# An adaLN block with a spectral filter: second layer norm's roots as a power on GpSimd, the Silu table loaded in the filter, one modulation later, one PSUM ring, a new order of the way back

## The chip, the cores and the metric

The kernel runs on one core of one Trainium2 chip. The metric is device time in microseconds of one execution; a kernel's time is the median of its runs. Before the change three runs gave 273.46, 274.78 and 277.28 us, median 274.78.

The engines by the profile's names: PE is TensorE's matmul, PEld its weight load, DVE is VectorE, ACT is ScalarE, POOL is GpSimd, SP issues nearly all transfers. Each engine works through its own instructions in order and waits for the others by semaphores.

## What is computed

One block on x of 2048 rows and 640 columns, in bf16, with six modulation vectors from a row c:

```python
mod = (_silu(c) @ w_mod).reshape(c.shape[0], 6, 1, -1)
sa, ca, ga, sb, cb, gb = ...
h = _layernorm(x, axis=-1) * (1 + ca) + sa
x = x + ga * _A_ref(h, A_w_r, A_w_i)     # irfft2(rfft2(h) * (w_r + 1j*w_i))
h = _layernorm(x, axis=-1) * (1 + cb) + sb
x = x + gb * _B_ref(h, B_w_gate, B_w_up, B_w_down)   # (silu(h@w_gate) * (h@w_up)) @ w_down
```

The layer norm has no weights: (x - m) / sqrt(v + 1e-5). The feed-forward is 1728 wide, that is 13 chunks of 128 and one half chunk of 64 (chunk 13 in the code).

## The kernel before

The 2048 rows lie on 128 partitions as 16 tiles. The stages follow one another: the first layer norm with the forward transforms (to about 36 us of the profile), the filter, 17 units of frequencies (to about 70 us), the way back, which overlaps with the second layer norm and the start of the feed-forward (to about 106 us), and the feed-forward in four blocks of four tiles (to the end).

Scheduling is by hand. In each stage a string of short words, `plan`, is walked and each word calls a step; every engine gets its instructions in the order of that string. For the way back (lines 799 to 805) the words are: `s` the inverse transform over rows of one tile on PE (L657, ten matmuls into `va`), `V` its copy to SBUF on ACT (L664), `d` the inverse transform over columns on PE (L670, five matmuls into `oab`), `x` the residual sum on DVE with its row sum (L673), `n` the mean on DVE (L677), `q` the square with its row sum on ACT (L681), `rt` the roots of tiles 0 to 3 (L683 to L687), `xn` and `xa` the normalised tile on DVE and ACT (L711, L714), `T` a pair of tiles turned on PE (L722), `f` its five affine pieces on ACT and DVE (L726, L728), `gA` chunk 13 (L749 and its Silu on ACT), `g`, `z`, `m` a chunk's ten matmuls (L762), its Silu on ACT (L767) and the product on DVE (L771), `mA` the product of chunk 13, `mb` and `mt` the columns of the gate gb and their turn into a row, `w` the fold of gb into a chunk of W_down on DVE (L788), `N` the roots of tiles 4 to 7, and `wm` the load of ACT's Silu table (L690).

Tiles 0 to 3 take their root as Sqrt on ACT and a reciprocal on DVE. The tiles behind them take it on DVE as an integer guess and three Newton steps, twelve short instructions (`ln2_newton`, L692 to L705). ACT holds one table of functions at a time: Silu is loaded at the start, Sqrt behind it (L358), Silu again at L690.

The modulations sb and cb are taken as columns on PE at the end of the filter (`mods_sb`, `mods_cb`, 25 matmuls of one column each, L221), and ACT writes them to `modcols` and `one_p_cb`; the affine pieces read both.

PSUM is a ring of four slots of two banks. The filter's pool, `ps2`, ends with the filter, and the way back has one of its own, `ps3`. A slot can be written again when the reader of the tile that held it four tiles earlier is done: a copy `V` for a `va`, a sum `x` for an `oab`, a product `m` for a chunk.

SBUF is shared by tags. W_gate (`Wg`) takes the place of `wm_g`, from which the columns of ga and cb are taken; `wm_gb` takes that of `wm_sb`; W_down (in `late`) takes that of the filter's weights `Wb`, which the products of the filter read. A transfer into such a place waits for the last reader of what was there. SP issues in this order at the end of the filter: `Wg` in two parts (L603), `wm_gb` (L629), W_down in three (L634, L636), later the turned gate's row to DRAM and its spread back to all partitions (L236, L242).

Of the kernel before, what the change touches and what calls it, by code (L numbers as in the profile page):

```python
# [104 lines left out]
def adaln_block_kernel(  # L105
# [28 lines left out]
    KIt = const.tile([P, 7, NI], BF16, name="KIt")  # L134
    modcols = const.tile([P, 2, NC5], F32, name="modcols")
# [270 lines left out]

    with tc.tile_pool(name="ph2", bufs=2) as ph2, \
         tc.tile_pool(name="ps2", bufs=4, space=bass.MemoryType.PSUM) as ps2:
        B2all = big.tile([P, 8, NR, 128], BF16, name="B2all", tag="gt")
# [162 lines left out]

        def rinv_gate(_):
# [13 lines left out]
        def loads(i):  # L587
            if i == 0:
                nc.sync.dma_start(wm_g[:, :, 0:D], wm_v[:, :, 2 * D:3 * D])
                nc.sync.dma_start(Rinv_sb[:], Rinv_dram)  # L590
            elif i == 1:
                nc.sync.dma_start(wm_g[:, :, D:2 * D], wm_v[:, :, 4 * D:5 * D])
            elif i == 2:
                nc.sync.dma_start(wm_sb[:], wm_v[:, :, 3 * D:4 * D])
            elif i == 3:
                nc.sync.dma_start(Htab[:], H_dram)
            elif i == 4:
                nc.sync.dma_start(Wu[:], B_w_up[:, 0:FFM].rearrange("(dp c5) f -> dp c5 f", dp=P))
                for k, w_ in enumerate((B_w_gate, B_w_up)):
                    nc.sync.dma_start(Wp13[:, :, 64 * k:64 * k + 64], w_[:, FFM:FF].rearrange("(dp c5) f -> dp c5 f", dp=P))  # L600
            else:
                for f0, f1 in ((0, 640), (640, FFM)):
                    nc.sync.dma_start(Wg[:, :, f0:f1], B_w_gate[:, f0:f1].rearrange("(dp c5) f -> dp c5 f", dp=P))  # L603

# [23 lines left out]
        wm_gb = big.tile([P, NC5, D], BF16, name="wm_gb", tag="wsb")
        nc.sync.dma_start(wm_gb[:], wm_v[:, :, 5 * D:6 * D])  # L629

    late = big.tile([P, NT * D + NFC * D], BF16, name="late", tag="wb")
# [44 lines left out]
    def ln2_mean(t):  # L676
        nc.vector.tensor_scalar(mean2[:, t:t + 1], xsum[:, t:t + 1], 1.0 / D, None, ALU.mult)  # L677

    def ln2_square(t):
        junk = ph4.tile([P, D], BF16, name="junk2", bufs=1)  # L680
        nc.scalar.activation(junk[:], x1[:, t, :], ACT.Square, scale=-1.0, bias=mean2[:, t:t + 1], accum_out=sq2[:, t:t + 1])  # L681

    def ln2_root(_):  # L683
        nc.scalar.activation(rstd2[:, 0:4], sq2[:, 0:4], ACT.Sqrt, bias=eps_t[:], scale=1.0 / D)
# [4 lines left out]
    def silu_table(_):  # L689
        nc.scalar.activation(warm[:], rstd2[:, 3:4], ACT.Silu)  # L690

    def ln2_newton(a, b):  # L692
        I32 = mybir.dt.int32
        n = b - a
        v = ph4.tile([P, 8], F32, name="veps")[:, 0:n]
        nc.vector.tensor_scalar(v, sq2[:, a:b], 1.0 / D, EPS, ALU.mult, ALU.add)
        yi = ph4.tile([P, 8], I32, name="rs_yi")[:, 0:n]
        nc.vector.tensor_single_scalar(yi, v.bitcast(I32), 1, ALU.arith_shift_right)
        nc.vector.tensor_scalar(yi, yi, -1, 0x5F3759DF, ALU.mult, ALU.add)
        y = yi.bitcast(F32)  # L700
        tt = ph4.tile([P, 8], F32, name="rs_t")[:, 0:n]
        for it in range(3):
            nc.vector.tensor_tensor(tt, y, y, ALU.mult)
            nc.vector.scalar_tensor_tensor(tt, tt, -0.5, v, ALU.mult, ALU.mult)
            nc.vector.scalar_tensor_tensor(rstd2[:, a:b] if it == 2 else y, tt, 1.5, y, ALU.add, ALU.mult)  # L705

    def ln2_xn(t):
        sc, tl = divmod(t, 4)
        if tl == 0 and sc:
            xn2s[sc] = big.tile([P, 4, D], BF16, name="xn2c", tag="rs")  # L710
        nc.vector.tensor_scalar(xn2s[sc][:, tl, :], x1[:, t, :], mean2[:, t:t + 1], rstd2[:, t:t + 1], ALU.subtract, ALU.mult)  # L711

# [64 lines left out]

    def gb_mods(_):
        mg_ps = ring("mg_ps")
        mod_cols(mg_ps[:, 0], wm_gb)  # L780
        nc.scalar.copy(g_col[1][:], mg_ps[:, 0, 0:NC5])

# [26 lines left out]

    done = 8  # L810
    folds = {8: (4, 5, 6), 9: (7,), 10: (8,), 11: (9, 10, 11), 12: (12, 13)}
    for sc in range(4):
# [139 lines left out]
```

## Time and profile before

| | us |
|---|---|
| median of three runs | 274.78 (273.46 to 277.28) |
| the profiled execution | 273.99 |
| its span, from the first instruction to the last | 272.2 |
| granted TensorE clock | 1.00 |

A stage's reading: busy time by engine in a stretch against its length. In a row of the timeline the first number is the start, the second the time from there to the end of the last of its instructions, and the bracket names the idle time of that engine just before and the instruction that ended it. Ends of matmuls are modelled and include a tail in which the next one already runs, so the rate of PE is read from starts. From 106 us on, the stretches look alike: a chunk every 2.16 us, then the products with W_down.

### The profile page before, as it was taken

Reading aid. Unit: us, or ns where it says so; the run is one execution under the profiler, and the core shown is the slowest. Engines: PE = TensorE matmul, PEld = TensorE weight load, DVE = VectorE, ACT = ScalarE, POOL = GpSimd, SP = SyncE. Lnnn points to the kernel's source line nnn. Section 1 sums busy time; section 2 is a strip of 40 time slices with the busy share of each in tenths; the row PEclk is TensorE's granted clock in tenths of the full one; section 3 lists DMA queues with packets and bytes.
Section 4 is the critical chain, followed back from the end, with each engine's and each line's share of the span. In section 5 each row is a group of like instructions: output and inputs, shape, how many; then the busy total and the mean of one; then the engine's idle time right before and its main releaser. Section 6 shows DMA issues by size and latency. Waiting matters only on the chain.

```text
span 272.2 us, 5350 instructions
## 1 busy us (share of the span) xinstructions
PE 260.6 (96%) x2190; PEld 169.0 (62%) x2190; DVE 151.0 (55%) x359; ACT 121.9 (45%) x221; POOL 22.0 (8%) x44
## 2 busy tenths in 40 slices
PE   6999989899987999999999999999999999999995
PEld 5888859798886555456744446654445664444663
DVE  2589989698577568892434553434334343333142
ACT  5499589798599985622032233022222203232000
POOL 3368910000000000000000000000000000000000
PEclk9999999999999999999999999999999999999999
DMA  7999359989499100031210005110004021000011
GB/s 241 333 327 276 131 106 246 281 203 287 102 377 355 29 11 26 0 63 37 72 35 12 0 0 96 51 55 3 12 0 88 11 72 34 12 0 0 0 52 48
DMA packets 35423, 27.80 MB, mean 102 GB/s; under 512 B 18117, under 2 KB 32710, under 8 KB 35270
## 3 DMA queue, kind: packets, MB, share of 16 engines
q1 hardware_dynamic: 35396, 27.46, 36.3%
q8 instruction: 17, 0.28, 0.4%
q14 instruction: 8, 0.07, 0.1%
q10 hardware_dynamic: 2, 0.00, 0.0%
HBM read 20.37 MB, written 2.62 MB: 84 GB/s over the span
## 4 chain that ended last, share of the span: by engine, by line
PE 78%; DMA 3%; ACT 3%; DVE 2%; issue 1%; SPq 0%; ACTq 0%; DVEq 0%
PE gu L762 41%; PE oa L863 20%; DMA wm_g<-in_w_mod_dram 3%; PE yps L493 2%; PE va L657 2%; PE gu L749 2%; DVE late L673 1%; PE m_ps L221 1%; PE oa L850 1%; PE oab L670 1%; PE wps L581 1%; ACT junk L681 1%; PE ob L863 1%; PE xps L446 1%; PE xps L447 1%
## 5 line engine op out<-in xcount | busy, mean ns | idle before, releaser
L771 DVE TENSOR_TENSOR AT<-gu,sg 128x512 bf16<-128x512 f32 x52 | 35.9, 690 | 54.4 <-ACT sg L767 54.4
L762 PE MATMUL gu<-h2T_all,Wg 128*128 128x512 bf16 x260 | 64.6, 380 | 0.0
L762 PE MATMUL gu<-h2T_all,Wu 128*128 128x512 bf16 x260 | 64.6, 380 | 0.0
L767 ACT ACTIVATE sg<-gu 128x512 f32<-128x512 f32 x52 | 31.0, 596 | 70.0 <-PE gu L762 68.5
L863 PE MATMUL oa<-late,AT 128*128 128x320 bf16 x403 | 56.1, 300 | 0.0
L863 PEld LDWEIGHTS <-AT 128*128 128x128 bf16 x429 | 40.8, 98 | 17.2 <-issue 1.4
L762 PEld LDWEIGHTS <-Wu 128*128 128x128 bf16 x260 | 25.4, 98 | 30.7
L762 PEld LDWEIGHTS <-Wg 128*128 128x128 bf16 x260 | 25.1, 98 | 29.4
L877 DVE TENSOR_TENSOR xo<-oa,late 128x320 bf16<-128x320 f32 x31 | 20.0, 695 | 29.3 <-PE oa L850 16.2
L673 DVE SCALAR_TENSOR_TENSOR late<-oab,x_sb 128x640 bf16<-128x640 f32 x16 | 14.1, 884 | 9.9 <-PE oab L670 9.8
L751 ACT ACTIVATE sg<-gu 64x512 f32<-64x512 f32 x4 | 2.3, 586 | 34.8 <-PE gu L749 34.8
L300 POOL TENSOR_SCALAR Gs<-Gtab,rstd 128x256 bf16<-128x256 bf16 x15 | 13.8, 922 | 12.3 <-DVE rstd L295 11.0
L312 DVE SCALAR_TENSOR_TENSOR Z<-rtile,vm,z 128x640 bf16<-128x640 f32 x16 | 13.9, 874 | 0.4 <-PE z L307 0.3
L681 ACT ACTIVATE junk<-late,mean 128x640 bf16<-128x640 bf16 x16 | 13.2, 827 | 0.3
L325 ACT CAST A_sb<-aps 128x650 bf16<-128x650 f32 x16 | 11.1, 706 | 2.5 <-PE aps L321 2.3
L276 ACT COPY early<-t1ps 128x640 bf16<-128x640 bf16 x13 | 9.0, 692 | 6.3 <-DVE ssq L285 3.1
L461 ACT CAST X<-xps 128x640 bf16<-128x640 f32 x16 | 10.9, 718 | 1.3 <-PE xps L454 0.6
L657 PE MATMUL va<-Htab,Ep 128*128 128x128 bf16 x160 | 10.7, 219 | 0.8 <-ACT VT L664 0.4
L664 ACT CAST VT<-va 128x640 bf16<-128x640 f32 x16 | 10.4, 701 | 1.4 <-PE va L657 1.4
L657 PEld LDWEIGHTS <-Ep 128*128 128x128 bf16 x160 | 9.9, 118 | 1.0 <-issue 0.8
L479 DVE TENSOR_TENSOR PP<-X,Wb 128x768 bf16<-128x768 bf16 x16 | 8.8, 552 | 2.7 <-ACT ga_col L559 2.3
L493 PE MATMUL yps<-identb,PP 128*128 128x128 bf16 x130 | 9.9, 219 | 0.3 <-ACT Y L504 0.3
(292 smaller groups left out, 340.9 us busy)
## 6 DMA issues: line engine op xcount, KB each, us to landing
x_sb<-in_A_x_dram SPq DMA_DIRECT2D x8, 320.0 KB, 5.8
out_dram<-xo SPq DMA_DIRECT2D x15, 160.0 KB, 1.8
Wu<-in_B_w_up_dram SPq DMA_DIRECT2D x1, 2080.0 KB
late<-in_B_w_down_dram SPq DMA_DIRECT2D x1, 2080.0 KB
wm_g<-in_w_mod_dram SPq DMA_DIRECT2D x2, 800.0 KB, 5.1
Wb<-in_A_w_r_dram SPq DMA_DIRECT2D x1, 1284.0 KB, 10.2
Wb<-in_A_w_i_dram SPq DMA_DIRECT2D x1, 1284.0 KB
Wg<-in_B_w_gate_dram SPq DMA_DIRECT2D x1, 1280.0 KB
```

Of the source, the lines that this page charges most:

```text
L300: e.tensor_scalar(Gss[t][:, 0:2], Gtab[:, t], rstd1[:, t:t + 1], None, ALU.mult)
L312: nc.vector.scalar_tensor_tensor(Zs[t][:].rearrange("p r q -> p (r q)"), rv, vm[:, t, 1:2], held.pop(("z", t))[:, 0:D], ALU.mult, ALU.add)
L325: (nc.vector.tensor_copy if t in A_DVE else nc.scalar.copy)(A_sb[:, :, t, :, :], i)
L493: nc.tensor.matmul(yf[:, 128 * j:128 * j + 128], lhsT=PP[:, cp, 0:128] if u == 16 else PP[:, cp, 0:128, j], rhs=identb[:], start=(cp == 0) ...
L657: nc.tensor.matmul(vf[:, 128 * r:128 * r + 128], lhsT=Ep[:, t, 65 - 65 * g:193 - 65 * g, r], rhs=Htab[:, t, g, :], start=(f == 1 and r in ...
L673: nc.vector.scalar_tensor_tensor(x1[:, t, :].rearrange("p (r a) -> p r a", r=NR), VTs.pop(t).rearrange("p (r a) -> p r a", r=NR), 1.0, x_s ...
L681: nc.scalar.activation(junk[:], x1[:, t, :], ACT.Square, scale=-1.0, bias=mean2[:, t:t + 1], accum_out=sq2[:, t:t + 1])
L762: nc.tensor.matmul(o, lhsT=w_[:, c5, fc * 128:(fc + 1) * 128], rhs=h2T_all[:, sc % 2, :, c5, :], start=(c5 == 0), stop=(c5 == NC5 - 1))
L767: nc.scalar.activation(gus[fc][1][:], gus[fc][0][:, 0, :], ACT.Silu)
L771: nc.vector.tensor_tensor(AT[:, fc, :], gu[:, 1, :], sg[:], ALU.mult)
L863: nc.tensor.matmul(o, lhsT=AT[:, fc, tl * 128:(tl + 1) * 128], rhs=Wd_sb[:, fc, h * 320 + d0:h * 320 + d0 + n], start=(fc == 0 and not ear ...
L877: nc.vector.tensor_tensor(xos[tl][:, h * 320:(h + 1) * 320].rearrange("p (a r) -> p a r", r=NR), ps[0][0].rearrange("p (a r) -> p a r", r= ...
```

## The change

Tiles 0 to 3, 4 to 7 and 8 to 15 get their roots from one step on GpSimd, an add of epsilon and a power with the exponent -0.5. So that the squares come out already divided by 640, the square's scale becomes -1/sqrt(640), and the mean is written twice, once as it is and once divided by sqrt(640), by one DVE instruction with a table `over_d`. The Silu table is loaded in the filter, ahead of the product of unit 6 and the columns of ga. The columns of sb and cb leave the filter's order; sb's come first in the way back, cb's behind the eighth `d`. The ring `ps2` stays for the rest of the kernel, and `ps3` goes. `wm_gb` is loaded behind sb's columns and `Wg` behind cb's, so that W_down is now ahead of both in SP's queue. The order of the way back is written anew. A copy of cb's columns that nothing read goes.

```diff
+    nc.gpsimd.memset(over_d[:, 0:1], 1.0 / D)
+    nc.gpsimd.memset(over_d[:, 1:2], D ** -1.5)
+    nc.gpsimd.memset(mhalf[:], -0.5)
...
-    with tc.tile_pool(name="ph2", bufs=2) as ph2, \
-         tc.tile_pool(name="ps2", bufs=4, space=bass.MemoryType.PSUM) as ps2:
+    ps2 = ctx.enter_context(tc.tile_pool(name="ps2", bufs=4, space=bass.MemoryType.PSUM))
+    with tc.tile_pool(name="ph2", bufs=2) as ph2:
...
-        def mods_cb(_):
-            m = mods(wm_g, 1)
-            nc.scalar.copy(modcols[:, 1, :], m)
-            nc.scalar.add(one_p_cb[:], m, 1.0)
-
-        def mods_sb(_):
-            nc.scalar.copy(modcols[:, 0, :], mods(wm_sb, 0))
+        def silu_table(_):
+            nc.scalar.activation(warm[:], eps_t[:], ACT.Silu)
...
-            "Xe9 P6 ga P7 Y4 Y5 y4 P8 y5 E3 X10 e3 Xe10 gt m0 E4 Y6 E5 y6 P9 Y7 e4 T16 W3 E6 e5 y7 t16 L4 X11 e6 E7 Y8 Xe11 "
+            "Xe9 wm P6 ga P7 Y4 Y5 y4 P8 y5 E3 X10 e3 Xe10 gt m0 E4 Y6 E5 y6 P9 Y7 e4 T16 W3 E6 e5 y7 t16 L4 X11 e6 E7 Y8 Xe11 "
...
-            "Xe15 Y13 Y16 y13 E10 E11 y16 P15 Y14 e10 E12 e11 y14 e12 E13 e13 Y15 E16 y15 m1 E14 m2 e16 E15 e14 m3 e15 m4 sb "
-            "Ri cb L5 "
+            "Xe15 Y13 Y16 y13 E10 E11 y16 P15 Y14 e10 E12 e11 y14 e12 E13 e13 Y15 E16 y15 m1 E14 m2 e16 E15 e14 m3 e15 m4 Ri "
...
-        wm_gb = big.tile([P, NC5, D], BF16, name="wm_gb", tag="wsb")
-        nc.sync.dma_start(wm_gb[:], wm_v[:, :, 5 * D:6 * D])
...
-    ps3 = ctx.enter_context(tc.tile_pool(name="ps3", bufs=4, space=bass.MemoryType.PSUM))
...
     def ln2_mean(t):
-        nc.vector.tensor_scalar(mean2[:, t:t + 1], xsum[:, t:t + 1], 1.0 / D, None, ALU.mult)
+        nc.vector.tensor_scalar(mean2[:, t], over_d[:], xsum[:, t:t + 1], None, ALU.mult)
 
     def ln2_square(t):
         junk = ph4.tile([P, D], BF16, name="junk2", bufs=1)
-        nc.scalar.activation(junk[:], x1[:, t, :], ACT.Square, scale=-1.0, bias=mean2[:, t:t + 1], accum_out=sq2[:, t:t + 1])
+        nc.scalar.activation(junk[:], x1[:, t, :], ACT.Square, scale=-1.0 / D ** 0.5, bias=mean2[:, t, 1:2], accum_out=sq2[:, t:t + 1])
+
+    def ln2_power(a, b):
+        nc.gpsimd.tensor_scalar(sq2[:, a:b], sq2[:, a:b], EPS, None, ALU.add)
+        nc.gpsimd.tensor_tensor(rstd2[:, a:b], sq2[:, a:b], mhalf[:, 0:b - a], ALU.pow)
 
     def ln2_root(_):
-        nc.scalar.activation(rstd2[:, 0:4], sq2[:, 0:4], ACT.Sqrt, bias=eps_t[:], scale=1.0 / D)
-        nc.vector.reciprocal(rstd2[:, 0:4], rstd2[:, 0:4])
-        nc.vector.scalar_tensor_tensor(nb2[:], mean2[:, 0:4], -1.0, rstd2[:, 0:4], ALU.mult, ALU.mult)
+        ln2_power(0, 4)
         xn2s[0] = big.tile([P, 4, D], BF16, name="xn2c", tag="rs")
...
+    def ln2_bias(_):
+        nc.vector.scalar_tensor_tensor(nb2[:], mean2[:, 0:4, 0], -1.0, rstd2[:, 0:4], ALU.mult, ALU.mult)
...
     plan = (
-        "s0 V0 s1 V1 s2 V2 s3 V3 s4 V4 d0 x0 n0 s5 V5 q0 d1 x1 n1 s6 q1 V6 d2 x2 s7 V7 d3 x3 n2 q2 n3 q3 d4 x4 s8 V8 d5 "
-        "x5 n4 n5 rt s9 V9 xn0 xn1 s10 V10 xa3 xn2 d6 T0 x6 s11 f0 V11 T1 f1 s12 V12 n6 d7 x7 n7 s13 V13 wm gA g0 q4 z0 "
-        "d8 x8 n8 m0 s14 V14 q5 g1 z1 d9 x9 n9 m1 s15 V15 q6 q7 g2 z2 d10 x10 n10 m2 mA mb q8 q9 g3 z3 d11 x11 n11 m3 "
-        "mt q10 g4 z4 d12 x12 n12 m4 d13 x13 n13 q11 w0 g5 z5 d14 x14 n14 m5 q12 d15 x15 n15 w1 g6 z6 m6 q13 w2 w3 q14 "
-        "g7 z7 m7 N q15 "
+        "sb s0 sx s1 V0 s2 d0 s3 x0 V1 s4 V2 d1 n0 d2 V3 s5 x1 V4 x2 q0 s6 d3 V5 n1 V6 d4 q1 s7 V7 x3 d5 n2 x4 q2 x5 mb "
+        "n3 d6 s8 s9 mx x6 d7 q3 rt x7 V8 n4 cb V9 nb s10 s11 xn2 xn0 cx V10 V11 d8 xa3 xn1 mt x8 T0 s12 T1 f0 s13 V12 f1 "
+        "d9 V13 s14 x9 n5 V14 s15 V15 d10 x10 gA n6 q4 q5 d11 d12 x11 g0 n7 d13 z0 x12 m0 w0 n8 n9 g1 q6 g2 q7 n10 z1 x13 "
+        "mA q8 q9 q10 w1 z2 d14 m1 g3 g4 n11 z3 x14 m2 n12 z4 q11 q12 n13 d15 x15 g5 m3 z5 n14 q13 m4 N g6 n15 q14 z6 q15 "
+        "w2 g7 m5 m6 w3 z7 m7 "
     )
     for w in plan.split():
         n = w.rstrip("0123456789")
         steps[n](int(w[len(n):] or 0))
+        if w == "sb":
+            wm_gb = big.tile([P, NC5, D], BF16, name="wm_gb", tag="wsb")
+            nc.sync.dma_start(wm_gb[:], wm_v[:, :, 5 * D:6 * D])
+        if w == "cb":
+            Wg = big.tile([P, NC5, FFM], BF16, name="Wg", tag="wg")
+            for f0, f1 in ((0, 640), (640, FFM)):
+                nc.sync.dma_start(Wg[:, :, f0:f1], B_w_gate[:, f0:f1].rearrange("(dp c5) f -> dp c5 f", dp=P))
```

In the new order `sx`, `cx` and `mx` are ACT's writes of sb, 1 + cb and gb, and `nb` is the bias for ACT's `xa`.

More of the change, by code (lines that the diff above doesn't have):

```diff
@@ L134, in adaln_block_kernel @@
     KIt = const.tile([P, 7, NI], BF16, name="KIt")
-    modcols = const.tile([P, 2, NC5], F32, name="modcols")
+    modcols = const.tile([P, 1, NC5], F32, name="modcols")
     one_p_cb = const.tile([P, NC5], F32, name="one_p_cb")
@@ L140, in adaln_block_kernel @@
     neg1 = const.tile([P, 1], F32, name="neg1")
+    over_d = const.tile([P, 2], F32, name="over_d")
+    mhalf = const.tile([P, 8], F32, name="mhalf")
     ssq, vm = (const.tile([P, NT, 2], F32, name=n) for n in ("ssq", "vm"))
@@ L600, in loads @@
                     nc.sync.dma_start(Wp13[:, :, 64 * k:64 * k + 64], w_[:, FFM:FF].rearrange("(dp c5) f -> dp c5 f", dp=P))
-            else:
-                for f0, f1 in ((0, 640), (640, FFM)):
-                    nc.sync.dma_start(Wg[:, :, f0:f1], B_w_gate[:, f0:f1].rearrange("(dp c5) f -> dp c5 f", dp=P))
         Y_ACT = (1, 3, 5, 7, 9, 11, 13, 15)
@@ L619, in adaln_block_kernel @@
                  "W": lambda i: negate(*WCOLS[i], neg_dve), "m": lambda i: mirror(*MCOLS[i]), "ga": mods_ga, "gt": ga_turn,
-                 "Ri": rinv_gate, "cb": mods_cb, "sb": mods_sb}
+                 "Ri": rinv_gate, "wm": silu_table}
         for w in plan.split():
@@ L624, in adaln_block_kernel @@
                 Wu = big.tile([P, NC5, FFM], BF16, name="Wu", tag="a")
-            if w == "L5":
-                Wg = big.tile([P, NC5, FFM], BF16, name="Wg", tag="wg")
             steps[n](int(w[len(n):] or 0))
-        wm_gb = big.tile([P, NC5, D], BF16, name="wm_gb", tag="wsb")
-        nc.sync.dma_start(wm_gb[:], wm_v[:, :, 5 * D:6 * D])
     late = big.tile([P, NT * D + NFC * D], BF16, name="late", tag="wb")
@@ L639, in adaln_block_kernel @@
     ph3 = ctx.enter_context(tc.tile_pool(name="ph3", bufs=6))
-    ps3 = ctx.enter_context(tc.tile_pool(name="ps3", bufs=4, space=bass.MemoryType.PSUM))
-    xsum, mean2, sq2, rstd2 = (const.tile([P, NT], F32, name=n) for n in ("xsum", "mean2", "sq2", "rstd2"))
+    xsum, sq2, rstd2 = (const.tile([P, NT], F32, name=n) for n in ("xsum", "sq2", "rstd2"))
+    mean2 = const.tile([P, NT, 2], F32, name="mean2")
     nb2 = const.tile([P, 4], F32, name="nb2")
@@ L645, in ring @@
     def ring(name):
-        return ps3.tile([P, 2, 512], F32, name=name, tag="f")
+        return ps2.tile([P, 2, 512], F32, name=name, tag="f")
     def flat(ps):
@@ L676, in ln2_mean @@
     def ln2_mean(t):
-        nc.vector.tensor_scalar(mean2[:, t:t + 1], xsum[:, t:t + 1], 1.0 / D, None, ALU.mult)
+        nc.vector.tensor_scalar(mean2[:, t], over_d[:], xsum[:, t:t + 1], None, ALU.mult)
     def ln2_square(t):
         junk = ph4.tile([P, D], BF16, name="junk2", bufs=1)
-        nc.scalar.activation(junk[:], x1[:, t, :], ACT.Square, scale=-1.0, bias=mean2[:, t:t + 1], accum_out=sq2[:, t:t + 1])
+        nc.scalar.activation(junk[:], x1[:, t, :], ACT.Square, scale=-1.0 / D ** 0.5, bias=mean2[:, t, 1:2], accum_out=sq2[:, t:t + 1])
+    def ln2_power(a, b):
+        nc.gpsimd.tensor_scalar(sq2[:, a:b], sq2[:, a:b], EPS, None, ALU.add)
+        nc.gpsimd.tensor_tensor(rstd2[:, a:b], sq2[:, a:b], mhalf[:, 0:b - a], ALU.pow)
     def ln2_root(_):
-        nc.scalar.activation(rstd2[:, 0:4], sq2[:, 0:4], ACT.Sqrt, bias=eps_t[:], scale=1.0 / D)
-        nc.vector.reciprocal(rstd2[:, 0:4], rstd2[:, 0:4])
-        nc.vector.scalar_tensor_tensor(nb2[:], mean2[:, 0:4], -1.0, rstd2[:, 0:4], ALU.mult, ALU.mult)
+        ln2_power(0, 4)
         xn2s[0] = big.tile([P, 4, D], BF16, name="xn2c", tag="rs")
[L689 to L705, printed above, removed]
+    def ln2_bias(_):
+        nc.vector.scalar_tensor_tensor(nb2[:], mean2[:, 0:4, 0], -1.0, rstd2[:, 0:4], ALU.mult, ALU.mult)
     def ln2_xn(t):
@@ L710, in ln2_xn @@
             xn2s[sc] = big.tile([P, 4, D], BF16, name="xn2c", tag="rs")
-        nc.vector.tensor_scalar(xn2s[sc][:, tl, :], x1[:, t, :], mean2[:, t:t + 1], rstd2[:, t:t + 1], ALU.subtract, ALU.mult)
+        nc.vector.tensor_scalar(xn2s[sc][:, tl, :], x1[:, t, :], mean2[:, t, 0:1], rstd2[:, t:t + 1], ALU.subtract, ALU.mult)
     def ln2_xa(t):
@@ L776, in ffn_mul13, with late_mods, sb_out, cb_out @@
         nc.sync.dma_start(AT[64:128, 13, :], AT[0:64, 13, :])
[L778 to L781, printed above, removed]
+    mod_ps = {}
+    def late_mods(name, w, k=0, strided=True):
+        mod_ps[name] = ring("mg_ps")[:, 0]
+        mod_cols(mod_ps[name], w, k, strided)
+    def sb_out(_):
+        nc.scalar.copy(modcols[:, 0, :], mod_ps["sb"][:, 0:NC5])
+    def cb_out(_):
+        nc.scalar.add(one_p_cb[:], mod_ps["cb"][:, 0:NC5], 1.0)
+    def gb_out(_):
+        nc.scalar.copy(g_col[1][:], mod_ps["mb"][:, 0:NC5])
     def gb_turn(_):
@@ L797, in adaln_block_kernel @@
              "T": pair_turn, "f": pair_affine, "gA": lambda _: ffn13(0), "g": lambda f: ffn_mm(0, f), "z": ffn_silu,
-             "m": lambda f: ffn_mul(AT2[0], f), "mA": lambda _: ffn_mul13(0, AT2[0]), "wm": silu_table, "N": lambda _: ln2_newton(4, 8), "mb": gb_mods, "mt": gb_turn, "w": fold}
+             "m": lambda f: ffn_mul(AT2[0], f), "mA": lambda _: ffn_mul13(0, AT2[0]), "N": lambda _: ln2_power(4, 8), "mb": lambda _: late_mods("mb", wm_gb, 0, False), "mx": gb_out, "mt": gb_turn,
+             "sb": lambda _: late_mods("sb", wm_sb), "sx": sb_out, "cb": lambda _: late_mods("cb", wm_g, 1), "cx": cb_out, "nb": ln2_bias, "w": fold}
     plan = (
[5 rows of a table removed]
[5 rows of a table added]
     )
@@ L825, in adaln_block_kernel @@
             if sc == 1 and fc == 4:
-                ln2_newton(8, 16)
+                ln2_power(8, 16)
             if sc < 3:
```

## The prediction

> **What bounds the kernel now.** I read the page's busy shares first, then a table by stage, then TensorE's rows inside the one stage that shows idle time, then the chain of waits there.
>
> ```profile
> PE 260.6 (96%) x2190; PEld 169.0 (62%) x2190; DVE 151.0 (55%) x359; ACT 121.9 (45%) x221; POOL 22.0 (8%) x44
> ```
>
> TensorE bounds the kernel, so an edit pays only where it closes one of TensorE's gaps. Busy time by stage (columns: stretch, its length, then busy time of PE, PEld, DVE, ACT, POOL, granted clock, DMA):
>
> ```profile
> 70.50:72.80 2.30, 1.99 (x51) 2.02 (x49) 1.67 (x4) 0.87 (x4) 0.00 (x0) 1.00 0.05 11
> 72.80:76.20 3.40, 3.38 (x61) 3.38 (x61) 0.05 (x1) 2.49 (x5) 0.00 (x0) 1.00 0.63 183
> 76.20:80.00 3.80, 3.02 (x50) 2.75 (x48) 3.73 (x13) 3.65 (x8) 0.00 (x0) 1.00 1.06 397
> 80.00:84.00 4.00, 2.55 (x44) 2.35 (x44) 2.92 (x11) 3.97 (x9) 0.00 (x0) 1.00 1.06 364
> 84.00:88.00 4.00, 3.71 (x57) 3.18 (x55) 3.38 (x11) 3.74 (x8) 0.00 (x0) 1.00 1.07 362
> 88.00:92.00 4.00, 4.00 (x31) 2.30 (x30) 2.04 (x7) 3.93 (x7) 0.00 (x0) 1.00 0.24 62
> ```
>
> From 88 us to the last chunk PE is never idle and the clock is 1.00. The gaps lie in the way back, 72 to 88 us, where ACT is full. The timeline's PE rows there (start, duration, then the idle time before in brackets):
>
> ```profile
> 79.09 0.44 PE L670 MATMUL oab<-Rinv_sb,VT 128*128 128x128 bf16 x5 [0.42 <-DVE late L673]
> 79.89 0.72 PE L657 MATMUL va<-Htab,Ep 128*128 128x128 bf16 x10 [0.36 <-ACT VT L664]
> ...
> 83.80 0.81 PE L722 MATMUL h2ps<-identb,xn2c 128*128 128x128 bf16 x10 [1.45 <-DVE xn2c L711]
> ...
> 86.52 0.44 PE L670 MATMUL oab<-Rinv_sb,VT 128*128 128x128 bf16 x5 [0.23 <-ACT VT L664]
> ```
>
> The bracket leaves out the modelled tail of each matmul. By starts alone, back-to-back work takes 0.56 us for a tile's ten `va` matmuls (84.45 to 85.01), 0.28 for the five `oab` (75.61 to 75.89), 2.16 for a chunk's ten `gu`. From `sb`'s start (70.37) to the end of the eighth chunk (sixth and seventh to eighth begin at 105.83; 105.83 + 2 x 2.16 = 110.15) pass 39.78 us. The work in it: 16 `va` 9.0, 16 `oab` 4.48, `sb` and `cb` 1.98, the gate's columns 0.60 and its turn 0.15, two pair turns 1.20, chunk 13 1.08, eight chunks 17.28: 35.77. So 4.0 us are gaps: 0.49 before the first `va`, 0.11, 0.58, 0.52, 0.07, then 1.61 before the first pair turn, 0.40 and 0.22. The chain of waits says whose they are:
>
> ```profile
> 80.33 0.94 ACT junk L681 x2
> 81.28 0.92 ACT junk L681 x2
> 82.21 0.58 ACT VT L664
> 82.78 0.20 ACT rstd L684
> ```
>
> The squares of tiles 2 and 3, then a copy, then the root: ACT decides when the first four tiles can be normalised.
>
> **The new order, walked.** I use the rows' spacing: a `VT` copy 0.60 (3.67 for six), a square with its read-out 0.95 (95.44 to 96.39), an `x1` sum 0.80, a mean 0.15, an `xn` 0.38, an affine piece 0.48 on ACT and 0.34 on DVE; 0.26 from PE's last issue to a reader, 0.05 otherwise. Walked so, the order of before ends its eighth chunk at 110.52 against 110.15 in the trace: 0.37 pessimistic.
>
> *One modulation later, one ring.* `sb` runs 70.3 to 71.35. The first `va` then needs only Ep: half of it the copy that ends at 71.56 (71.06 + 0.50), half the last mirror (71.60 + 0.32 = 71.92), so it ends at 72.25, against 73.40 before (72.82 + 0.58), where `cb` and the ring's first slot (0.33 behind ACT `one_p_cb`) stood in front. `cb` (0.98) is not saved: it now stands behind the eighth `oab`, at 80.8.
>
> *ACT up to the square of tile 3.* From 72.5: eight copies 4.8, four squares 3.8, `gb_col` 0.15, a wait of 0.16: 81.4. In the trace of before the fourth square's read-out ends at 82.2. PE meanwhile does `va` 0 to 9, `oab` 0 to 7 and the gate's columns, with gaps of 0.26, 0.08, 0.23, 0.03, 0.04, 0.09 and 0.28: 1.0.
>
> *The roots on GpSimd.* Away go ACT's Sqrt (0.30) and DVE's reciprocal (0.18); in come an add and a power of 128x4 on POOL, which has nothing else after 36 us. No row has a power. The lower bound is a tiny POOL instruction (0.09, the memset of one element), the upper one the Newton root on DVE, the same value in twelve short steps: 2.4 us (149.13 to 151.50). The nearest POOL rows are these, 0.37 for 128 elements a partition:
>
> ```profile
> 9.80 0.93 POOL L300 TENSOR_SCALAR Gs<-Gtab,rstd 128x256 bf16<-128x256 bf16 x1 [6.80 <-DVE rstd L295]
> 10.71 0.37 POOL L301 TENSOR_SCALAR Gs<-Gtab,rstd 128x128 bf16<-128x128 bf16 x1
> ```
>
> I take 0.1 for the add and 0.4 for the power, being of that engine. Then `nb2` ends at 82.2, the three `xn` on DVE at 83.4; behind `nb2` on DVE stand the `xn`, for which the first pair turn waits, and the ninth sum, whose slot the second pair turn takes. PE fills that time with `cb`, two `va`, an `oab` and the gate's turn (gaps 0.20 and 0.04) and is free for the pair turn at 83.66, so the root has some 0.6 us of cover: it costs nothing up to about 1.1 in all, and beyond that microsecond for microsecond.
>
> *To the feed-forward.* The second pair waits 0.26 for ACT's `xn` of tile 3, a sum 0.04 and a `va` 0.32 for the affine pieces and copy 12 on ACT. Chunk 13 starts at 88.20. Behind it: 1.08 + five `oab` 1.40 + eight chunks 17.28 = 107.96, no gap, as each chunk's slot was emptied at least 0.4 us before. Gaps in all 1.87.
>
> So the gain is 39.78 - (107.96 - 70.30) = 2.1, or 2.55 by walk against walk. I take 2.3.
>
> *Silu table in the filter.* These rows give its price and its place:
>
> ```profile
> 51.23 0.17 ACT L559 CAST ga_col<-m_ps 128x5 bf16<-128x5 f32 x1 [1.04 <-PE m_ps L221]
> ...
> 88.49 1.28 ACT L690 ACT_TABLE_LOAD   x1
> ...
> 89.78 0.20 ACT L690 ACTIVATE warm<-rstd 128x1 f32<-128x1 f32 x1
> ```
>
> ACT is idle from 50.19 to 51.23, waiting for PE, which waits for `wm_g`. The load (1.28) and its activation (0.10 to the next start) push `ga_col` to 51.6; the next copy starts at 52.38 and the gate's turn at 53.45, so it costs nothing. Uncovered it would be 1.4. What it leaves at 88.49 was off the path: PE has no gap there. [...]
>
> *SP's queue.* Three loads change places. Before:
>
> ```profile
> 72.52 1.22 SPq L603 DMA_DIRECT2D Wg<-in_B_w_gate_dram  x2
> 73.79 0.63 SPq L629 DMA_DIRECT2D wm_gb<-in_w_mod_dram  x1
> 74.46 1.00 SPq L634 DMA_DIRECT2D late<-in_B_w_down_dram  x1
> ```
>
> W_down goes first, free at 67.1 when the last product has read Wb; Wu still flows till 69.7. At 0.38 MB/us (78 to 80 us) its 2.29 MB end near 75.5, `wm_gb` (issued 71.5, 0.82 MB) near 78, wanted at 78.15 with 0.7 to spare. Wg leaves with `cb` at 81.9; 800 KB take about 5 (5.1 for `wm_g`), so 87, wanted at 89.84; the rest by 92, wanted past 101. Behind Wg stand the gate's row and spread; DVE first needs them at its first fold near 94, and a spread by 92 leaves room. All cost nothing.
>
> *Newton's steps* (2.4 us of DVE each, with PE gapless) and a `modcols` copy go: nothing. The larger power calls have over 10 us of cover: tiles 4 to 7 are rooted at 95 and read after 112.
>
> **The sum.** The profiled execution took 273.99 for a span of 272.2; less 2.3 it is 271.7. The median shown is 0.79 higher, 274.78; on that footing 272.5. The 2% that a measurement of this kernel can tell from no change are 5.5 us.
>
> **Rivals.** *The root becomes the wait.* At Newton's 2.4 us it outlasts its cover by 1.4: 273.9. For it: a power is no plain arithmetic. Against: POOL is idle and the input is tiny.
>
> *The loads come late.* In the trace `wm_gb` took 10.8 from issue to landing. From 71.5 that is 82.3: 4.1 after its turn, less 0.7 cover, 3.4 lost: 275.9. For it: it would share the rings with W_down. Against: before, 2.1 MB of Wg were ahead and W_down beside it; now nothing follows for 10 us.
>
> *Slower: a lane-by-lane power on POOL.* At `ln2_power(0, 4)` everything of the first pair waits. From 3.4 us (1.1 + 2.3) the change loses; from 8.9 it is 2% slower. Twice Newton, 4.8 (a logarithm and an exponential, my estimate), gives 276.2. For it: nothing in the trace bounds a POOL function; against: no POOL row is above 0.97.
>
> *POOL fetches code at the first power.* Once only, at that same place; the nearest load of tables is ACT's 1.28, which with 0.5 outlasts the cover by 0.7: 273.2. [...] Here the first scale on POOL took 0.93 and the median one 0.92, so no such cost shows.
>
> *It closes all gaps:* 4.0, so 270.8. ACT's sum speaks against it. *The new order only moves them:* 274.8, if DVE's sums (0.89 busy each) hold up the ring.
>
> **Chances.** Forecast 0.52; root as the wait 0.12; late loads 0.07; lane by lane 0.11; code 0.05; all gaps closed 0.05; gaps only moved 0.08. Range 270.0 (all gaps closed, with scatter) to 276.2 (late loads and the doubled Newton). Faster by over 2% needs more than the gaps hold, so scatter alone: 0.05. Slower by over 2%: most of the lane-by-lane case and a slow fetch, 0.10. Within: 0.85.
>
> **What would show it.** The `va` of tile 0 ends near 72.3; the fourth square at 81.4; the power under 1 us; the first pair turn near 83.7; chunk 13 at 88.2; the eighth chunk's end near 108; ACT's load beside PE's wait at 50 us. A power row above 1 us, a PE wait for `wm_gb` or Wg, or a DVE wait at the first fold would show a step wrong.

## The result, and the profile after

| | before | after |
|---|---|---|
| median of 20 runs each, us | 274.46 (272.59 to 277.28) | 276.89 (274.12 to 279.22) |
| the profiled execution, us | 273.99 | 277.17 |
| its span, us | 272.2 | 275.4 |
| granted TensorE clock in it | 1.00 | 0.985 |

The change makes the kernel slower by 0.6%: the ratio is 1.0058, with a 95% interval of 1.0034 to 1.0082. The ratio leaves out the slow runs, those over 1.5% above the fastest of their kernel (five after, one before), and so is smaller than that of the medians shown. The forecast was 272.5, with a range from 270.0 to 276.2.

The page's busy share and the granted clock in 40 slices of the kernel after:

```profile
PE 262.7 (95%) x2190; PEld 170.6 (62%) x2190; DVE 147.5 (54%) x334; ACT 122.1 (44%) x219; POOL 27.3 (10%) x53
...
PEclk9999999999995999999999999999999999999998
```

PE has as many instructions as before and 2.1 us more of busy time, and one slice stands at half clock. It lies in the way back; the stretches of the prediction (length, then PE, PEld, DVE, ACT, POOL, granted clock, DMA share, GB/s):

```profile
70.50:72.80 2.30, 2.17 (x44) 2.05 (x43) 1.85 (x5) 0.64 (x2) 0.00 (x0) 1.00 1.07 363
72.80:76.20 3.40, 3.40 (x65) 3.40 (x63) 1.80 (x4) 3.30 (x6) 0.00 (x0) 1.00 1.08 344
76.20:80.00 3.80, 2.27 (x38) 1.98 (x36) 3.80 (x13) 3.80 (x9) 0.00 (x0) 1.00 0.66 203
80.00:84.00 4.00, 2.80 (x54) 2.80 (x55) 1.03 (x3) 1.92 (x7) 0.82 (x2) 0.85 0.01 4
84.00:88.00 4.00, 4.00 (x55) 3.80 (x52) 2.23 (x7) 1.91 (x4) 0.46 (x1) 0.50 0.30 67
88.00:92.00 4.00, 3.94 (x54) 3.70 (x54) 2.34 (x7) 3.69 (x8) 0.00 (x0) 0.80 1.04 387
```

Up to 76 us PE is nearly always busy (5.57 of 5.70 us). Then it stands still, and from 84 to 88 it is busy all the time at half speed: 55 matmuls, against 79 in 81 to 85 us of the first experiment below, which has no such wait. PE's rows on the timeline name the wait:

```profile
78.19 0.44 PE L661 MATMUL oab<-Rinv_sb,VT 128*128 128x128 bf16 x5
81.20 0.78 PE L226 MATMUL mg_ps<-sc_col,wm_gb 128*128 128x1 bf16 x25 [2.57 <-DMA wm_gb<-in_w_mod_dram]
...
85.18 2.31 PE L648 MATMUL va<-Htab,Ep 128*128 128x128 bf16 x20
...
88.15 1.25 PE L700 MATMUL h2ps<-identb,xn2c 128*128 128x128 bf16 x10
```

All that PE does next stands in its order behind the 25 columns of the gate, and their weights land at 81.15. Behind them, twenty `va` take 2.31 us; at full clock such a group takes 1.28 (75.64 in the same profile). The chain of waits steps over the whole of it by one transfer:

```profile
71.80 9.36 DMA wm_gb<-in_w_mod_dram
81.15 0.05 issue
81.20 0.78 PE mg_ps L226 x25
```

From `sb`'s start to the end of the eighth chunk pass 42.52 us (70.64 to 113.16), against 39.78 before and 37.66 forecast (107.96 - 70.30).

A second loss lies where nothing was forecast, at the end of the first transforms. POOL's and PE's rows after:

```profile
33.12 1.52 POOL L306 TENSOR_SCALAR Gs<-Gtab,rstd 128x128 bf16<-128x128 bf16 x1
...
34.70 0.31 PE L326 MATMUL aps<-Z,Gs 128*128 128x315 bf16 x1 [1.16 <-POOL Gs L306]
```

and the same POOL instruction before, for which PE did not wait:

```profile
33.74 0.37 POOL L301 TENSOR_SCALAR Gs<-Gtab,rstd 128x128 bf16<-128x128 bf16 x1
```

The last tile's scaling of the transform's table is four times as long. The change edits nothing in this stage; only the three memsets of `over_d` and `mhalf` are new on POOL ahead of it, at 2.8 us. The measure used below is the time from the last reciprocal of this stage (DVE `rstd`) to the start of `sb`'s columns, since the reciprocal itself moves with the first loads (31.3 to 33.0 us in the profiles): 37.94 before (32.43 to 70.37), 39.18 after (31.46 to 70.64).

So the 3.2 us between the two profiled spans are 2.74 in the way back, 1.24 at this place, less 0.97 by which the reciprocal came earlier in this execution, and 0.2 behind the eighth chunk, whose cause is open.

### The profile page after: what moved, and what is told of

It is laid out like the page before. It is cut to its first block, busy times and chain, and to the rows that moved or that the text cites. A ratio compares the mean times of both kernels' runs of the same rounds, so it can differ in the third digit from the quotient of the medians.

```text
span 275.4 us, 5331 instructions
## 1 busy us (share of the span) xinstructions
PE 262.7 (95%) x2190; PEld 170.6 (62%) x2190; DVE 147.5 (54%) x334; ACT 122.1 (44%) x219; POOL 27.3 (10%) x53
## 4 chain that ended last, share of the span: by engine, by line
PE 79%; DMA 3%; ACT 2%; DVE 1%; issue 0%; ACTq 0%
PE gu L740 41%; PE oa L859 20%; DMA wm_gb<-in_w_mod_dram 3%; PE yps L498 2%; PE va L648 2%; PE gu L727 2%; PE oab L661 1%; PE mg_ps L226 1%; PE oa L846 1%; PE xps L451 1%; PE wps L581 1%; PE xps L452 1%; PE ob L859 1%; PE yps L502 1%; ACT Y L509 1%; PE t2ps L431 1%
## 5 line engine op out<-in xcount | busy, mean ns | idle before, releaser
L648 PE MATMUL va<-Htab,Ep 128*128 128x128 bf16 x160 | 12.2, 238 | 0.2
L648 PEld LDWEIGHTS <-Ep 128*128 128x128 bf16 x160 | 11.1, 124 | 0.4 <-DVE Ep L543 0.2
L326 PE MATMUL aps<-Z,Gs 128*128 128x315 bf16 x32 | 9.2, 299 | 1.2 <-POOL Gs L306 1.2
```

What stands on the lines that cost most here:

```text
L648: nc.tensor.matmul(vf[:, 128 * r:128 * r + 128], lhsT=Ep[:, t, 65 - 65 * g:193 - 65 * g, r], rhs=Htab[:, t, g, :], start=(f == 1 and r in ...
```

## The experiments

Theory: the late `wm_gb` costs its wait and then the clock, while the new order itself gains. Rivals: the root on GpSimd (1.37 us, not 0.5) is what makes the way back long; the clock falls for another reason; the order itself doesn't gain. "Way back" below is the time from `sb`'s start to the end of the eighth chunk in the profile (42.52 after), "first stage to filter's end" the measure above.

**W_down's loads behind `wm_gb`.**

```diff
-    nc.sync.dma_start(Wd_sb[:, 0:13, :], B_w_down[0:FFM, :].rearrange("(fc fp) d -> fp fc d", fp=P))
-    for o in (0, 64):
-        nc.sync.dma_start(Wd_sb[o:o + 64, 13, :], B_w_down[FFM:FF, :])
...
             nc.sync.dma_start(wm_gb[:], wm_v[:, :, 5 * D:6 * D])
+            nc.sync.dma_start(Wd_sb[:, 0:13, :], B_w_down[0:FFM, :].rearrange("(fc fp) d -> fp fc d", fp=P))
+            for o in (0, 64):
+                nc.sync.dma_start(Wd_sb[o:o + 64, 13, :], B_w_down[FFM:FF, :])
```

> W_down's three loads are issued behind wm_gb instead of ahead of it; all else is the changed kernel. Theory A (PE's 2.57 us wait for wm_gb, and the half clock that follows it from 82.8 to 89.3, are the whole loss): wm_gb lands by 78, PE does not wait for it, the granted clock stays at 1.00, and the time is 2 to 2.5 us under the kernel before (ratio 0.991 to 0.993). Theory B (the clock falls for another reason in the new order, or the roots' 1.37 us on POOL are the loss): the wait is gone but the clock is still below 0.99 or the pair turn still late, and the time stays above 0.998 of before.

Measured 273.39 us, ratio 0.9976 (0.9943 to 1.0009). The way back falls to 38.04, 4.48 under after and 1.74 under before. PE's rows of the timeline, to be held against those of after:

```profile
78.80 0.44 PE L658 MATMUL oab<-Rinv_sb,VT 128*128 128x128 bf16 x5
79.08 0.77 PE L226 MATMUL mg_ps<-sc_col,wm_gb 128*128 128x1 bf16 x25
...
84.38 0.73 PE L697 MATMUL h2ps<-identb,xn2c 128*128 128x128 bf16 x10
```

and the stretch of its table that is set against the half clock of after:

```profile
81.00:85.00 4.00, 4.00 (x79) 3.83 (x77) 3.40 (x10) 3.58 (x8) 1.28 (x2) 1.00 0.70 195
```

No wait for the weights, and the clock stays at 1.00. The 800 KB of `wm_gb`, with W_down behind them, land in 4.7 us instead of 9.36. Nor does PE wait for the root: the pair turn follows the gate's turn (84.23) at once. By the way back the new order does gain. The time gains less than expected, and its interval does not leave out 1: the wait for POOL in the first stage is here too (first stage to filter's end 39.12).

**The gate's columns later in the order**, with the loads as they were.

```diff
-... x4 q2 x5 mb n3 d6 s8 s9 mx x6 ... xn1 mt x8 T0 ...
+... x4 q2 x5 n3 d6 s8 s9 x6 ... xn1 mb x8 T0 s12 T1 f0 mx s13 V12 f1 d9 V13 mt s14 ...
```

> The gate's columns are taken behind the ninth oab instead of behind the sixth, the transfers keep the changed kernel's order. Theory A: wm_gb has landed (81.2) before its turn near 83.5, no wait, clock 1.00; PE has a gap of about 0.9 us near 78.5 where the columns stood, part of it given back behind, so 1.3 to 2.5 us under before (0.991 to 0.995). Theory B: above 0.998, with the clock below 0.99.

Measured 273.51, ratio 0.9976 (0.9951 to 1.0001); way back 38.22, at a clock of 1.00. The same result, again less than expected in time, without touching a transfer: what hurt was who stood behind the late weights on PE. But the clock did fall elsewhere in this profile, as the page's 40 slices show (the second and the sixth):

```profile
PEclk9799979999999999999999999999999999999999
```

The second fall, at 36.7 us, makes first stage to filter's end 40.12. The last section comes back to it.

**Work in the gap.** 44 matmuls that nobody reads, ahead of the gate's columns, in the slot they are given anyway.

```diff
-        mod_ps[name] = ring("mg_ps")[:, 0]
+        mg = ring("mg_ps")
+        for _ in range(44 if name == "mb" else 0):
+            nc.tensor.matmul(mg[:, 1, 0:128], lhsT=identb[:], rhs=identb[:], start=True, stop=True)
+        mod_ps[name] = mg[:, 0]
```

> 44 matmuls of 128 columns into the unused bank of the gate's slot stand ahead of its columns: they add work that nothing reads. The wait for wm_gb is as long as before, but PE works through it. If an idle PE is what halves the clock: clock 1.00 (0.99 and up), and the 3.2 us lost at the half clock come back, so 0.5 to 1.2 us under before (ratio 0.995 to 0.999). If the clock is taken for another reason (Theory B): clock near 0.985 and a ratio of 1.004 or more.

Measured 275.41, ratio 1.005 (1.0014 to 1.0085); way back 40.13. By PE's rows the columns start when they did after:

```profile
78.78 2.62 PE L761 MATMUL mg_ps<-identb 128*128 128x128 bf16 x44
81.23 0.77 PE L226 MATMUL mg_ps<-sc_col,wm_gb 128*128 128x1 bf16 x25
```

and by the busy time in two stretches the clock holds:

```profile
83.00:84.00 1.00, 1.00 (x25) 1.00 (x23) 0.54 (x3) 1.00 (x3) 0.80 (x2) 1.00 0.00 0
84.00:89.00 5.00, 4.58 (x83) 4.29 (x82) 3.41 (x11) 4.08 (x10) 0.48 (x1) 1.00 0.58 169
```

The kernel after has 0.50 in both stretches, with 12 and 64 matmuls. So the clock is 42.52 - 40.13 = 2.39 us of the way back, and the wait by itself 40.13 - 38.04 = 2.09. The ratio misses the expected 0.995 to 0.999: the clock gave back 2.39 us and not 3.2, and the 1.2 us of the first stage are lost here too. The unprofiled executions bear out the profiles: the mean clock over a whole execution was 1.00 in seven of these ten, and in none of the twenty of after (0.973 to 0.998). There the two highest, 0.998 and 0.997, belong to the two shortest times, 274.12 and 274.65 us. Half clock for 6.8 us would alone take the mean to 0.988, so the wait does not halve the clock in every execution.

**Only the two loads of 80 KB behind `wm_gb`** (W_down's last half chunk, loaded twice).

```diff
-    for o in (0, 64):
-        nc.sync.dma_start(Wd_sb[o:o + 64, 13, :], B_w_down[FFM:FF, :])
...
             nc.sync.dma_start(wm_gb[:], wm_v[:, :, 5 * D:6 * D])
+            for o in (0, 64):
+                nc.sync.dma_start(Wd_sb[o:o + 64, 13, :], B_w_down[FFM:FF, :])
```

> Only the two 80 KB loads of W_down's last chunk go behind wm_gb; the 2 MB load stays ahead. If the tail of wm_gb (bulk traffic ends at 78.6, it lands at 81.1) comes from these two: it lands near 78.5, the wait is under 0.5 us, clock 1.00 and the ratio as in e1, 0.991 to 0.994. If it comes from the bulk load: the wait stays above 1.5 us and the ratio near 1.005.

Measured 275.52, ratio 1.0021 (0.9976 to 1.0065): the time can't tell. PE's row of its profile can:

```profile
80.23 0.78 PE L226 MATMUL mg_ps<-sc_col,wm_gb 128*128 128x1 bf16 x25 [1.28 <-DMA wm_gb<-in_w_mod_dram]
```

Half the wait goes with these 160 KB, so neither expectation was met. Their bytes alone would take 0.45 us at the 363 GB/s of the table above, and every packet of W_down and `wm_gb` in the trace has 1280 bytes; why they cost 1.29 is open, and so is the other half. In this profile a wait of 1.28 leaves the clock at 1.00. Way back 39.13.

**The three memsets alone, in the kernel before.** Why all these gain some 1.2 us less than the way back says was tested next.

```diff
+    nc.gpsimd.memset(over_d[:, 0:1], 1.0 / D)
+    nc.gpsimd.memset(over_d[:, 1:2], D ** -1.5)
+    nc.gpsimd.memset(mhalf[:], -0.5)
```

> The kernel before, with nothing of the change but its three new memsets on POOL (two columns of over_d, and mhalf), whose results nobody reads. In the changed kernel and in the four experiments so far POOL's last scaling of the transforms' tables took 1.5 us instead of 0.37, and PE waited 1.2 us for it ahead of the last tile's transform. [...] Theory B, the wait comes from something else in the changed program, or from chance: no PE wait above 0.3 us there in this profile, ratio 1.000.

Measured 276.53, ratio 1.0053 (1.0019 to 1.0088), with nothing else of the change in it; way back 39.80, as before. POOL's last two scalings in its profile:

```profile
32.03 0.92 POOL L305 TENSOR_SCALAR Gs<-Gtab,rstd 128x256 bf16<-128x256 bf16 x1 [1.08 <-DVE Gs L306]
32.93 1.53 POOL L306 TENSOR_SCALAR Gs<-Gtab,rstd 128x128 bf16<-128x128 bf16 x1
```

PE waits 1.2 us for it, and first stage to filter's end is 39.41. DVE's rows from the last reciprocal on:

```profile
31.29 0.16 DVE L300 RECIPROCAL rstd<-rstd 128x2 f32<-128x2 f32 x1
...
32.70 0.82 DVE L388 TENSOR_TENSOR dsa<-t1ps,identb 5x650 bf16<-5x650 f32 x1
33.44 0.83 DVE L259 TENSOR_SCALAR Wb<-Wb,neg 128x816 bf16<-128x816 bf16 x2
```

**The same three on VectorE,** with W_down behind `wm_gb`.

```diff
-    nc.gpsimd.memset(over_d[:, 0:1], 1.0 / D)
-    nc.gpsimd.memset(over_d[:, 1:2], D ** -1.5)
-    nc.gpsimd.memset(mhalf[:], -0.5)
+    nc.vector.memset(over_d[:, 0:1], 1.0 / D)
+    nc.vector.memset(over_d[:, 1:2], D ** -1.5)
+    nc.vector.memset(mhalf[:], -0.5)
```

> The changed kernel with W_down's loads behind wm_gb (as in e1_down_behind, 273.39 us), and with the same three memsets on VectorE instead of POOL, so that POOL's instructions ahead of the way back are those of the kernel before. Theory A (the memsets cause the wait at the last tile): the last scaling takes 0.37 us on POOL, PE does not wait for it, and the time falls by about 1.2 us, to 272.2, ratio about 0.993. Theory B: the wait of 1.2 us stays, ratio 0.997.

Measured 272.11, ratio 0.9896 (0.984 to 0.9952); way back 38.04, first stage to filter's end 37.89. The same two POOL rows:

```profile
32.12 0.92 POOL L305 TENSOR_SCALAR Gs<-Gtab,rstd 128x256 bf16<-128x256 bf16 x1 [0.84 <-DVE rstd L300]
33.01 0.37 POOL L306 TENSOR_SCALAR Gs<-Gtab,rstd 128x128 bf16<-128x128 bf16 x1
```

and DVE's rows beside them:

```profile
31.70 0.16 DVE L300 RECIPROCAL rstd<-rstd 128x2 f32<-128x2 f32 x1
31.95 0.29 DVE L305 TENSOR_SCALAR Gs<-Gtab,rstd 128x256 bf16<-128x256 bf16 x1
32.16 0.48 DVE L306 TENSOR_SCALAR Gs<-Gtab,rstd 128x128 bf16<-128x128 bf16 x1
```

POOL waits for that reciprocal, and DVE goes on behind it. Here POOL starts 0.42 after the reciprocal's start, ahead of DVE's second scaling, which is stretched (0.48 instead of 0.25). With the three memsets on POOL it starts 0.74 after it (31.29 to 32.03 above), behind both (0.29 and 0.25), and so its short scaling runs into DVE's `dsa` and the two negations of `Wb`: it lasts until 34.46, 0.19 past their end. Which of them holds it up, and how, is argued from this overlap and not shown by an experiment. What the rows show are lengths: the same POOL instruction takes 0.37 or 1.53, the same DVE one 0.25 or 0.48. DVE's stretched scaling ends at 32.64, while POOL's, begun before it, runs to 33.04, so there the later one did not wait for the end of the earlier.

The time gains about 1 us more than the two measures, which give 1.79. The mean clock of whole executions points at the rest: 1.00 in three of these four, but in only five of the 19 of the kernel before beside them (0.994 or 0.988 in the others). That was not tested.

**The last tile's scaling on VectorE too,** memsets left on POOL, W_down behind.

```diff
-        HT_DVE, A_DVE, S_DVE, T_RING = (0,), (), (14,), (1, 3)
+        HT_DVE, A_DVE, S_DVE, T_RING = (0,), (), (14, 15), (1, 3)
```

> The changed kernel with W_down's loads behind wm_gb, and with the last tile's scaling of its table (two instructions, 0.29 and 0.25 us on VectorE) on VectorE instead of POOL. Whichever way POOL came to be late, its last two scalings are gone from the end of that stage: if the 1.2 us that PE waits there are lost for good, the time falls by about 1.2 us to 272.2 (ratio 0.993), with no wait of PE for POOL in the stage. Rival: VectorE is as late with its own chain there (0.5 us more on it, and the last Z and the spectrum's sums behind it), so that PE waits for VectorE instead, and the time stays at 273.4 (ratio 0.997).

Measured 272.41, ratio 0.9898 (0.9835 to 0.996); PE waits for POOL nowhere in the stage, and first stage to filter's end is 38.14, against 39.12 in the first experiment: of DVE's extra half microsecond at most 0.25 is left there (38.14 - 37.89). Two different remedies of the same 1.2 us end at the same time within the noise of four runs each.

**The first power twice,** W_down behind, memsets on POOL.

```diff
-        nc.gpsimd.tensor_tensor(rstd2[:, a:b], sq2[:, a:b], mhalf[:, 0:b - a], ALU.pow)
+        for _ in range(2 if a == 0 else 1):
+            nc.gpsimd.tensor_tensor(rstd2[:, a:b], sq2[:, a:b], mhalf[:, 0:b - a], ALU.pow)
```

> The changed kernel with W_down's loads behind wm_gb, and with the first power on GpSimd (128x4, 1.04 us in the profiles) done twice in a row. If the root has no cover left (its 1.37 us were sized at 0.5 against a cover of about 1.1), the whole second power lands on the time: from the filter's end to the end of the eighth chunk 39.1 us instead of the 38.04 of e1_down_behind, time 274.4, ratio about 1.001. If PE's other work still covers it, less than 0.4 us: ratio 0.998.

Measured 274.48, ratio 0.9985 (0.9955 to 1.0014); way back 38.61, that is 0.57 more for 1.09 more on POOL, between the two expectations. POOL's row with the two powers:

```profile
81.77 2.13 POOL L674 TENSOR_TENSOR rstd<-sq,mhalf 128x4 f32<-128x4 f32 x2
```

and PE's rows behind it:

```profile
84.87 0.81 PE L698 MATMUL h2ps<-identb,xn2c 128*128 128x128 bf16 x10 [0.85 <-DVE xn2c L687]
...
89.42 0.44 PE L658 MATMUL oab<-Rinv_sb,VT 128*128 128x128 bf16 x5 [0.22 <-ACT VT L652]
```

The pair turn now waits 0.85 and comes 0.92 later after `sb`'s start (14.04 against 13.12), and a later wait for ACT's copy (0.48 with one power) is gone: 0.35 is given back. With one power the root ends just in time, with 0.17 (1.09 - 0.92) to spare.

**Which memsets do it.** One, six, and three placed behind the scaling on POOL, all with W_down behind `wm_gb`. The first and the third against the first experiment; the second gives the three lines twice:

```diff
-    nc.gpsimd.memset(over_d[:, 0:1], 1.0 / D)
-    nc.gpsimd.memset(over_d[:, 1:2], D ** -1.5)
+    nc.vector.memset(over_d[:, 0:1], 1.0 / D)
+    nc.vector.memset(over_d[:, 1:2], D ** -1.5)
     nc.gpsimd.memset(mhalf[:], -0.5)
```

```diff
-    nc.gpsimd.memset(over_d[:, 0:1], 1.0 / D)
-    nc.gpsimd.memset(over_d[:, 1:2], D ** -1.5)
-    nc.gpsimd.memset(mhalf[:], -0.5)
...
         nc.gpsimd.memset(PP64[:], 0.0)
+        nc.gpsimd.memset(over_d[:, 0:1], 1.0 / D)
+        nc.gpsimd.memset(over_d[:, 1:2], D ** -1.5)
+        nc.gpsimd.memset(mhalf[:], -0.5)
```

> As e6_memsets_dve, but with one of the three memsets (mhalf, 0.10 us) left on POOL at the start. [...]

> As e1_down_behind (three memsets on POOL at the start), but with each of the three given twice, so six on POOL. Theory A1 (any further POOL instruction ahead): the last scaling takes 1.5 us and PE waits 1.2 us, as with three. Theory A2 (where the instructions come to lie in the stream): with six the wait may be gone again, 0.37 us and no wait.

> As e1_down_behind, but with the three memsets on POOL behind its last scaling and the padding's memset instead of at the start: as many POOL instructions, none of them new ahead of the scaling. Theories A1 and A2 alike: the last scaling takes 0.37 us, PE does not wait for it, the way from the last reciprocal of the stage to the filter's end is 1.2 us shorter than in e1_down_behind. If the wait stays, the place of the memsets is not the cause, but the length of POOL's program.

One execution each, 272.92, 271.90 and 272.06 us; the scaling takes 0.37 in all three, without a wait of PE for it, and first stage to filter's end is 37.84, 37.88 and 37.85. With three at the start, and the scaling on POOL, it took 1.51 to 1.53 in all seven profiles; with none, one or six it did in none. So "any further instruction on POOL" falls: with six there are more. What in their position makes POOL late by 0.3 us stays open.

**All remedies together,** W_down behind, memsets on VectorE, the last scaling on VectorE.

> [...] Theory: the remedies overlap (each takes away the same 1.2 us), so it stands where e6_memsets_dve and e7_last_scale_dve stood, 272.2 us, ratio 0.990. Rival: what the two take away adds, 271.2 us, ratio 0.986.

Measured 272.40, ratio 0.9917 (0.9888 to 0.9947): faster than both kernels (the median of after is 276.89), and the remedies overlap.

## Why the prediction was wrong, point by point

**The step that failed: "`wm_gb` (issued 71.5, 0.82 MB) near 78, wanted at 78.15 with 0.7 to spare".** It was issued at 71.80 and landed at 81.15. SP's queue after:

```profile
67.35 0.39 SPq L625 DMA_DIRECT2D late<-in_B_w_down_dram  x1
67.78 3.11 SPq L627 DMA_DIRECT2D late<-in_B_w_down_dram  x2
71.80 0.39 SPq L800 DMA_DIRECT2D wm_gb<-in_w_mod_dram  x1
```

and the stretches before the weights land, whose last two columns are the DMA's busy share and its GB/s:

```profile
78.00:79.00 1.00, 0.63 (x12) 0.46 (x9) 1.00 (x4) 1.00 (x3) 0.00 (x0) 1.00 0.49 164
79.00:80.00 1.00, 0.00 (x0) 0.00 (x0) 1.00 (x5) 1.00 (x3) 0.00 (x0) 1.00 0.10 33
80.00:81.00 1.00, 0.00 (x0) 0.00 (x0) 0.12 (x1) 0.22 (x2) 0.00 (x0) 1.00 0.04 15
```

Nearly all bytes were done when the sum said, at 78 to 79; then a tail of 48 KB took two more microseconds (33 and 15 GB/s for one each), in which on average fewer than two of the 16 DMA engines were busy (shares of 0.10 and 0.04). Here a size divided by a rate gave the end of the bulk, not the landing of the last packet, some 2 us later. Of the 160 KB of the half chunk that stood ahead, 0.45 us was counted by their bytes, and they cost 1.29 of the wait; what makes the tail is open. The 10.8 us that the same load took in the trace of before was the better guess. The rival "the loads come late" (0.07) was the right mechanism, 82.3 against 81.15.

**What neither the forecast nor that rival priced: the clock.** The rival took the wait beyond a cover of 0.7 microsecond for microsecond. The wait of 2.57 cost 2.09 so, a cover of 0.48, and 2.39 more through 6.8 us at half clock (82.8 to 89.6), which began 1.6 us after work had begun again. Together 4.48, against 0 in the sum and 3.4 in the rival.

**A term that the sum lacked: the three memsets.** They were not in it at all. They cost 1.2 to 1.5 us 30 us later, and alone make the kernel before 0.5% slower, about as much as the whole change.

**The new order: right in kind, 0.56 short.** Without the late load it gains 1.74 of the 2.3 taken (39.78 - 38.04). The pair turn comes 13.13 us after `sb`'s start, forecast 13.36 (83.66 - 70.30); chunk 13 at 18.30, forecast 17.90. So 0.63 is lost between them, where the walk had "a `va` 0.32 for the affine pieces and copy 12 on ACT"; with the memsets on VectorE PE's row there reads

```profile
85.60 0.44 PE L658 MATMUL oab<-Rinv_sb,VT 128*128 128x128 bf16 x5 [0.48 <-ACT VT L652]
```

and the `oab` of the next tile waits another 0.22.

**The root: wrong in size, right in cost.** POOL's rows after:

```profile
83.09 0.24 POOL L675 TENSOR_SCALAR sq<-sq 128x4 f32<-128x4 f32 x1 [47.33 <-ACT junk L672]
83.42 1.04 POOL L676 TENSOR_TENSOR rstd<-sq,mhalf 128x4 f32<-128x4 f32 x1
```

1.37 in all where 0.1 and 0.4 were taken and "up to about 1.1" called free. In the first experiment it costs PE nothing; the doubled power shows that about half of the next microsecond would have landed. A first call dearer than a later one was not seen: the first power starts 0.09 behind the add, and the second call of 128x4 took 1.04 as well. That POOL's first scaling took 0.93, on which the prediction set this cost aside, says little: it stood behind 6.80 us of idle time, which could hide such a cost. The slow fetch in the prediction's chance of "slower by over 2%" is shown by no run.

**The Silu table in the filter: right.** ACT's rows after:

```profile
50.47 1.28 ACT L571 ACT_TABLE_LOAD   x1
51.77 0.20 ACT L571 ACTIVATE warm<-eps_t 128x1 f32<-128x1 f32 x1
51.88 0.15 ACT L564 CAST ga_col<-m_ps 128x5 bf16<-128x5 f32 x1
```

`ga_col` at 51.9 (forecast 51.6), the next copy 0.49 idle behind it. The activation starts 0.02 behind the load. In both kernels ACT loads a table three times, for Silu, Sqrt and Silu again, 1.28 us each: at 1.28, 2.86 and 88.49 before, at 1.26, 2.84 and 50.47 after.

**Wg and the gate's spread: right.** Issued 3.4 us later than forecast (85.35), the 800 KB landed in 5.0 us, and neither PE nor the first fold waited.

## What to carry to other kernels

Where a load stands in front of work that can't be reordered, plan with a landing measured in the trace under the same traffic, not with bytes over a rate, and ask what the wait does to TensorE's clock: here, in the profiled executions, a wait of 2.57 us cost 4.48, while one of 1.28 left the clock alone. Where two engines wait for the same instruction, an edit elsewhere in their programs can change how long one of them takes: here, with three memsets of 0.1 us at the start, POOL's last two scalings began 0.3 us later against DVE's, and the last took 1.53 instead of 0.37 us. So give such work to one engine: with the last tile's scaling on VectorE, PE waited for POOL nowhere in the stage. When experiments give less than they should by the same amount, look for the rest in the stages that were not edited.

## What the runs showed of the hardware

TensorE's clock fell to 0.50 after a wait of 2.57 us in after (from about 78.6 to 81.2), while single waits of 1.28 us in the fourth experiment and 1.45 us before left it at 1.00; it fell only when PE was at work again, at 82.8, and came back at 89.6.

The length of one wait does not decide by itself. In the profile of the second experiment the clock fell for about 3.4 us at 36.7 (a mean of 0.88 from 36 to 50 us), behind waits of 1.16 and 0.79. The same two waits, 1.16 and 0.79, left it at 1.00 in after, and 1.19 and 0.79 did in the first experiment. What else decides is not shown. In the other twelve profiles the mean clock over the whole execution is 0.998 or 1.00. Before 13 us the clock's rows say little: in the profiles of before, after and the first four experiments the first matmuls run at about half the later rate (in after five of 128x128 take 0.53 us from start to start at 9.92, and 0.28 at 14.31) until 11 to 13 us, in the second experiment with a break from about 7.4 to 9.4. Yet in the other five the clock reads 1.00 from 5 to 10 us.

On GpSimd a power of 128x4 elements in f32 took 1.04 us in after, one of 128x8 1.67, an add of 128x4 0.24. In the kernel before, three memsets of 0.1 us, none of whose results is read there, made the time 1.0053 times as long.
